# Rewriting the start of a fused retention and mixing kernel: order of the first batch's work on each engine, and idle products in TensorE's waits

## Chip, cores, metric

One core of one Trainium2 chip. The metric is the device time of one execution in microseconds (us). Executions come in states: the state "slow" is given to a run more than 1.5% above the fastest of the same kernel. For this kernel the states go with TensorE's granted clock (the share of full speed that the profile shows for it, 1 being full).

## The reference, cut to what matters

```python
# part 1: retention, B=4, H=8 heads, S=768, D=64, a state per head
state = gamma * state + k_t v_t^T ;  x_t = scale * q_t state
# part 2: x is (B, 768, 512)
theta = x @ w_theta
zr, zi = x * cos(theta), x * sin(theta)
u = x + w_tok_r @ zr + w_tok_i @ zi      # over the 768 positions
out = u + relu(u @ w_ch)
```

The kernel computes part 1 in chunks of 128 positions, 6 to a batch, 24 in all, and part 2 in tiles of 128 positions, each of which needs all six chunks of its batch.

## The kernel before: the parts in question

The first batch is special, because nothing is there yet: its six chunks are loaded and computed as three pairs (pair g = chunks 2g, 2g+1), while the weights still arrive. The helpers below say which engine does what. In the traces each of the engines that compute starts its operations in the order of these calls, even if a later one has its data: in the kernel before, pair 1's k has landed at 13.4 us, but ScalarE casts it at 17.24, after two copies that stand ahead of it.

```python
def pair_prep(g, name):     # cast / scale to bf16
    # k: ScalarE, one copy of 128x1024; q: VectorE and GpSimd, half each; v: GpSimd twice
def pair_T(g, name):        # 8 TensorE transposes into PSUM (tag "tr", 2 buffers)
    nc.vector.tensor_copy(t, ps)                     # kqT
def pair_A(g, two):         # 16 score products into at_ps (1 buffer), then
    nc.vector.tensor_mul(at, at_ps, maskp)           # masked scores
def pair_S(g, a):           # 8 products: k^T v into the state; ScalarE copies it (stbd)
def pair_I(g, a):           # 4 products: q times the state
def pair_Y(g, two):         # 16 products: scores times v
def pair_out(g, a):         # ScalarE copies yT to xT
def att_X(n):               # 4 transposes (x_sb), 4 products theta, ScalarE cos and sin
def att_Z(n):               # VectorE: z = (cos, sin) * x
def w_cast(t0): ...         # GpSimd casts two rows of w_tok (wrow, 3 buffers)
def w_tok(t0): ...          # 12 transposes, copies on VectorE (wtr) and ScalarE (wti)
def moe_M(m, lo, hi): ...   # tile m: 2 products of 128x512 for each chunk lo..hi-1
```

The schedule of the first two pairs (the third follows the same way, with the first tiles' products between):

```python
for _ in range(14):                                   # opening: TensorE kept busy
    nc.tensor.matmul(warm_ps, warm[:, 0:P], warm, start=True, stop=True)
pair_k(0); pair_q(0)                                  # pair_k = pair_prep + pair_T
pair_prep(0, "v"); pair_A(0, 0)
nc.gpsimd.tensor_copy(wth, wdma["th"])
pair_A(0, 1); pair_S(0, 0); pair_Y(0, 0); pair_S(0, 1); pair_I(0, 1); pair_Y(0, 1)
pair_out(0, 0); pair_out(0, 1)
pair_k(1); att_X(0); pair_q(1); att_X(1); att_Z(0)
pair_prep(1, "v"); pair_A(1, 0); att_Z(1); w_cast(0); pair_A(1, 1)
pair_S(1, 0); pair_Y(1, 0); pair_I(1, 0); pair_I(1, 1); pair_S(1, 1); pair_Y(1, 1)
pair_out(1, 0); pair_out(1, 1)
pair_prep(2, "k"); att_X(2); att_X(3); w_tok(0); pair_T(2, "k"); moe_M(0, 0, 2)
... (cut)
```

Of the kernel before, what the change touches and what calls it, by code (L numbers as in the profile page):

```python
# [32 lines left out]
def kernel(  # L33
# [17 lines left out]
    nc = tc.nc  # L51
    B, H, S, D = q.shape
    dm = H * D
    P = 128
# [38 lines left out]
    wdma = {}  # L93
# [90 lines left out]
    def att_prep(n):  # L184
        c = n % nT
        r3 = "p (h d) -> p h d"
        kqb = work.tile([P, 2, dm], BF, name="kqb", bufs=5)
        kb, qb = kqb[:, 0, :], kqb[:, 1, :]
        vb = work.tile([P, dm], BF, name="vb", bufs=5)
        nc.gpsimd.tensor_copy(kb.rearrange(r3, h=H), raw[n, "kf"])  # L190
        nc.gpsimd.tensor_mul(qb.rearrange(r3, h=H), raw[n, "qf"],  # L191
                             _bcast_last(qsc[:, c], D))
        nc.gpsimd.tensor_mul(vb.rearrange(r3, h=H), raw[n, "vf"],  # L193
                             _bcast_last(vsc[:, c], D))
        st[n] = dict(kqb=kqb, kb=kb, qb=qb, vb=vb)
# [20 lines left out]
    def pair_prep(g, name):  # L216
        t = work.tile([P, 2, dm], BF, name="kqb", bufs=5)
        src = raw[g, name].rearrange("p h (two d) -> p two h d", two=2)
        dst = t.rearrange("p two (h d) -> p two h d", h=H)
        if name == "k":  # L220
            nc.scalar.copy(dst, src)
        for two in range(2):
            if name == "q":
                eng = (nc.vector, nc.gpsimd)[two]
                eng.tensor_mul(dst[:, two], src[:, two],
                               _bcast_last(qscp[:, 2 * g + two], D))
            elif name == "v":
                nc.gpsimd.tensor_mul(dst[:, two], src[:, two],
                                     _bcast_last(vscp[:, 2 * g + two], D))
        st[g, name] = t  # L230

    def pair_T(g, name):
        ps = psum.tile([P, NP, 2, P], BF, name="kq_ps", tag="tr", bufs=2)
        for two in range(2):
            for j in range(NP):
                nc.tensor.transpose(ps[:, j, two, :],  # L236
                                    st[g, name][:, two, j * P:(j + 1) * P], ident)
        t = work.tile([P, NP, 2, P], BF, name="kqT", bufs=4)
        nc.vector.tensor_copy(t, ps)
        st[g, name + "T"] = t  # L240

    def pair_A(g, two):

        at_ps = psum.tile([P, 2, NP, P], FT, name="at_ps", tag="at", bufs=1)
        kT, qT = st[g, "kT"], st[g, "qT"]
        for j in range(NP):
            for a in range(2):
                half = slice(a * HP, (a + 1) * HP)
                for par in range(2):
                    rows = slice(par * D, (par + 1) * D)  # L250
                    nc.tensor.matmul(at_ps[half, par, j, :], kT[rows, j, two, half],
                                     qT[rows, j, :, half], start=(j == 0),
                                     stop=(j == NP - 1), skip_group_check=True)
        at = work.tile([P, 2, NP, P], BF, name="at", bufs=2)
        nc.vector.tensor_mul(at.rearrange("p a j t -> p (a j) t"),  # L255
                             at_ps.rearrange("p a j t -> p (a j) t"),
                             _bcast_mid(maskp[:, two].rearrange("p w i -> p (w i)"), H))
        st[g, two] = at

    def pair_Y(g, two):  # L260

        if two == 0:
            st[g, "y"] = [psum.tile([P, NP, P], FT, name="yT_ps", tag="acc", bufs=2)
                          for _ in range(2)]
        yT, at, vp = st[g, "y"], st[g, two], st[g, "v"]
        for j in range(NP):
            for a in range(2):
                half = slice(a * HP, (a + 1) * HP)
                for par in range(2):
                    h = 2 * j + par  # L270
                    nc.tensor.matmul(yT[a][par * D:(par + 1) * D, j, :],
                                     vp[half, two, h * D:(h + 1) * D],
                                     at[half, par, j, :],
                                     start=(two == 0 and j == 0),
                                     stop=(two == 1 and j == NP - 1),
                                     skip_group_check=True)

    def pair_I(g, a):

        c = 2 * g + a  # L280
        half = slice(a * HP, (a + 1) * HP)
        yT = st[g, "y"][a]
        if c > 0:
            for j in range(NP):
                nc.tensor.matmul(yT[:, j, :], stbd[c % 2][:, j, :],
                                 st[g, "qT"][:, j, :, half], start=False,
                                 stop=False, skip_group_check=True)

    def pair_out(g, a):
        c = 2 * g + a  # L290
        yT = st[g, "y"][a]
        if c == 0:
            x_tiles(0)
        xT = work.tile([P, NP, P], BF, name="xT", bufs=3)
        nc.scalar.copy(xT.rearrange("e j (i w) -> e j w i", w=2),
                       yT.rearrange("e j (w i) -> e j w i", w=2))
        st[c] = dict(xT=xT)

    def pair_S(g, a):

        c = 2 * g + a
        half = slice(a * HP, (a + 1) * HP)
        if c == 0:
            st_ps[0] = psum.tile([P, NP, P], FT, name="st_ps", tag="st", bufs=1)
        for two in range(2):
            for j in range(NP):
                nc.tensor.matmul(st_ps[0][:, j, :],  # L307
                                 st[g, "k"][half, two, j * P:(j + 1) * P],
                                 st[g, "v"][half, two, j * P:(j + 1) * P],
                                 start=(c == 0 and two == 0 and j == 0),  # L310
                                 stop=(c == nT - 2 and two == 1 and j == NP - 1),
                                 skip_group_check=True)
        state_out(0, c)
# [90 lines left out]
    def att_Z(n):  # L404
        b, c = divmod(n, nT)
        nc.vector.tensor_mul(zs[b][:, c], st[n]["cs"], _bcast_mid(xs[b][:, c, :], 2))  # L406
# [57 lines left out]
    def w_cast(t0):  # L464
        for r in range(2):
            row = work.tile([P, S], BF, name="wrow", bufs=3)
            nc.gpsimd.tensor_copy(row, wdma[r, t0])  # L467
            wrow[r, t0] = row

    def w_tok(t0):  # L470
        for r in range(2):
            w_ps = psum.tile([P, nT, P], BF, name="w_ps", tag="tr", bufs=2)
            for s0 in range(nT):
                nc.tensor.transpose(w_ps[:, s0, :],
                                    wrow[r, t0][:, s0 * P:(s0 + 1) * P], ident)
            dst = wT[r][:, :, t0 * P:(t0 + 1) * P]
            if r:
                nc.scalar.copy(dst, w_ps)  # L478
            else:
                nc.vector.tensor_copy(dst, w_ps)  # L480
# [50 lines left out]
    def pair_k(g):  # L531
        pair_prep(g, "k")
        pair_T(g, "k")

    def pair_q(g):
        pair_prep(g, "q")
        pair_T(g, "q")


    warm_ps = psum.tile([P, dm], FT, name="y_ps", tag="y", bufs=1)  # L540
    for _ in range(14):
        nc.tensor.matmul(warm_ps, warm[:, 0:P], warm, start=True, stop=True)  # L542

    pair_k(0)
    pair_q(0)
    pair_prep(0, "v")
    pair_A(0, 0)
    nc.gpsimd.tensor_copy(wth, wdma["th"])
    pair_A(0, 1)
    pair_S(0, 0)  # L550
    pair_Y(0, 0)
    pair_S(0, 1)
    pair_I(0, 1)
    pair_Y(0, 1)
    pair_out(0, 0)
    pair_out(0, 1)
    pair_k(1)
    att_X(0)
    pair_q(1)
    att_X(1)  # L560
    att_Z(0)
    pair_prep(1, "v")
    pair_A(1, 0)
    att_Z(1)
    w_cast(0)
    pair_A(1, 1)
    pair_S(1, 0)
    pair_Y(1, 0)
    pair_I(1, 0)
    pair_I(1, 1)  # L570
    pair_S(1, 1)
    pair_Y(1, 1)
    pair_out(1, 0)
    pair_out(1, 1)
    pair_prep(2, "k")
    att_X(2)
    att_X(3)
    w_tok(0)
    pair_T(2, "k")
    moe_M(0, 0, 2)  # L580
    pair_q(2)
    att_Z(2)
    pair_prep(2, "v")
    pair_A(2, 0)
    moe_M(0, 2, 3)
    att_Z(3)
    w_cast(1)
    pair_A(2, 1)
    pair_S(2, 0)
    pair_Y(2, 0)  # L590
    pair_I(2, 0)
    pair_I(2, 1)
    moe_M(0, 3, 4)
    pair_Y(2, 1)
    pair_out(2, 0)
    pair_out(2, 1)
    w_tok(1)
    att_X(4)
    w_cast(2)
    att_prep(nT)  # L600
    moe_M(1, 0, 4)
    att_X(5)
    att_Z(4)
    moe_M(0, nT - 2, nT - 1)
    moe_M(1, nT - 2, nT - 1)
    att_T(nT)
    att_Z(nT - 1)
    w_tok(2)
    moe_M(0, nT - 1, nT)
    moe_M(1, nT - 1, nT)  # L610

# [4 lines left out]
    for m in range(2, nT):  # L616
        i = 2 * (m - 2)
# [88 lines left out]
```

## Time and profile before

| | before |
|---|---|
| runs, us | 188.95, 226.11, 191.99, 189.16: median 190.57 |
| span of the profiled run (a further one, 191.03 us, fast) | 189.3 us |
| mean granted TensorE clock of it | 0.955 |
| TensorE busy, share of the span | 88% |
| first scores of the loop (chunk 6) begin | 55.96 us |
| from there to the end | 133.3 us |

Up to chunk 6's scores lies the code that the change rewrites, from there on the code is the same in both kernels. From about 70 us on TensorE is busy nearly without gaps (between 56 and 72 us it is busy for 13.7 of 16). In the first 56 us it waits, and its clock is halved for 17 us.

### The profile page before, as it was taken

To read this page: it belongs to the slowest core of one execution; us is meant where nothing else is said; L and a number is where in the kernel's file an instruction comes from. 1 tells how busy PE (TensorE), PEld (TensorE's weight loads), DVE (VectorE), ACT (ScalarE), POOL (GpSimd) and SP (SyncE) were. 2 spreads that over 40 slices of the span, in tenths; PEclk is the share of its full clock that TensorE was granted. 3 is DMA by queue.
4 is the path that set the end of the run, shared out by engine and by line. 5 is a ranking of instruction groups with operands and counts; after the bars stand their busy time and mean duration, and the time that the engine had idled before them with its cause. 6 is when DMAs were issued, how large, how long until landed. Compare 5 with 4: busy or idle time off the path is not lost.

```text
span 189.3 us, 3807 instructions
## 1 busy us (share of the span) xinstructions
PE 166.2 (88%) x1496; PEld 95.6 (51%) x1522; DVE 106.5 (56%) x150; ACT 78.9 (42%) x146; POOL 73.1 (39%) x102
## 2 busy tenths in 40 slices
PE   7645966869878969999999999999999999999991
PEld 2333544445445645565556655555555544444560
DVE  2360690482368558787875768665656544443442
ACT  6316247515414683564636453554454532200010
POOL 6375390304499879865552267205000000000000
PEclk9985596978999999999999999999999999999999
DMA  4999999299999999999989579992384334244343
GB/s 143 318 317 336 292 357 209 68 256 253 240 225 282 216 223 212 263 277 207 235 143 214 134 148 220 207 194 73 66 155 110 89 68 111 83 139 112 96 132 113
DMA packets 85907, 35.65 MB, mean 188 GB/s; under 512 B 70912, under 2 KB 80384, under 8 KB 85888
## 3 DMA queue, kind: packets, MB, share of 16 engines
q1 hardware_dynamic: 85744, 35.27, 79.8%
q8 instruction: 12, 0.20, 0.5%
q10 hardware_dynamic: 144, 0.13, 0.2%
q14 instruction: 7, 0.06, 0.1%
HBM read 25.69 MB, written 6.29 MB: 169 GB/s over the span
## 4 chain that ended last, share of the span: by engine, by line
PE 79%; DVE 8%; ACT 5%; issue 4%; DMA 2%; DVEq 0%; ACTq 0%
PE y_ps L424 29%; PE o_ps L452 10%; PE th_ps L395 10%; PE yT_ps L359 3%; PE at_ps L330 3%; PE y_ps L542 3%; PE kq_ps L202 3%; PE x_ps L392 3%; PE st_ps L367 2%; PE kq_ps L236 2%; PE st_ps L307 2%; DVE at L255 2%; PE yT_ps L348 2%; PE u_ps L435 2%; DMA uT<-u 2%
## 5 line engine op out<-in xcount | busy, mean ns | idle before, releaser
L424 PE MATMUL y_ps<-z,wti 128*128 128x512 bf16 x135 | 51.2, 379 | 1.0 <-ACT wti L478 0.2
L424 PE MATMUL y_ps<-z,wtr 128*128 128x512 bf16 x126 | 48.0, 381 | 1.4 <-DVE z L406 1.0
L400 ACT ACTIVATE cs<-th_ps,halfpi 128x512 bf16<-128x512 f32 x24 | 16.5, 687 | 38.8 <-PE th_ps L395 36.4
L406 DVE TENSOR_TENSOR z<-cs,x_sb 128x1024 bf16<-128x1024 bf16 x24 | 19.0, 793 | 15.1 <-ACT cs L401 15.1
L395 PE MATMUL th_ps<-wth,xT 128*128 128x512 bf16 x89 | 26.0, 402 | 0.7 <-issue 0.4
L334 DVE TENSOR_TENSOR at<-at_ps,mask 128x1024 bf16<-128x1024 f32 x18 | 22.0, 1221 | 6.3 <-PE at_ps L330 6.2
L452 PE MATMUL o_ps<-wch,uT 128*128 128x512 bf16 x88 | 23.1, 379 | 0.4 <-DMA uT<-u 0.2
L429 DVE TENSOR_TENSOR u<-y_ps,x_sb 128x512 bf16<-128x512 f32 x23 | 15.8, 690 | 12.0 <-PE y_ps L424 12.0
L455 DVE SCALAR_TENSOR_TENSOR ot<-o_ps,u 128x512 f32<-128x512 f32 x23 | 15.9, 692 | 10.5 <-PE o_ps L452 10.4
L193 POOL TENSOR_TENSOR vb<-vf,vsc 128x512 bf16<-128x512 f32 x18 | 19.2, 1065 | 6.3 <-PE yT_ps L359 3.6
L318 ACT CAST stbd<-st_ps 64x256 bf16<-64x256 f32 x40 | 14.6, 366 | 16.6 <-PE st_ps L307 16.1
L424 PEld LDWEIGHTS <-wti 128*128 128x128 bf16 x138 | 13.5, 98 | 15.8 <-issue 2.8
L424 PEld LDWEIGHTS <-wtr 128*128 128x128 bf16 x138 | 13.5, 98 | 13.3
L191 POOL TENSOR_TENSOR kqb<-qf,qsc 128x512 bf16<-128x512 f32 x18 | 19.6, 1086 | 1.0 <-DMA qf<-in_q_dram 1.0
L190 POOL CAST kqb<-kf 128x512 bf16<-128x512 f32 x18 | 11.4, 635 | 19.6 <-issue 10.4
L467 POOL CAST wrow<-wtok 128x768 bf16<-128x768 f32 x12 | 9.8, 824 | 19.3 <-issue 18.9
L401 ACT ACTIVATE cs<-th_ps,zerob 128x512 bf16<-128x512 f32 x24 | 16.3, 679 | 0.0
L375 ACT CAST xT<-yT_ps 128x512 bf16<-128x512 f32 x18 | 10.5, 585 | 8.7 <-PE yT_ps L359 7.4
L452 PEld LDWEIGHTS <-uT 128*128 128x128 bf16 x92 | 8.8, 98 | 10.2 <-DMA uT<-u 0.4
L395 PEld LDWEIGHTS <-xT 128*128 128x128 bf16 x96 | 9.3, 105 | 7.8 <-issue 1.8
L205 DVE COPY kqT<-kq_ps 128x1024 bf16<-128x1024 bf16 x13 | 9.0, 690 | 6.7 <-PE kq_ps L202 6.7
L398 DVE COPY x_sb<-x_ps 128x512 bf16<-128x512 bf16 x19 | 7.9, 417 | 7.2 <-PE x_ps L392 7.2
(78 smaller groups left out, 198.7 us busy)
## 6 DMA issues: line engine op xcount, KB each, us to landing
out_dram<-ot SPq DMA_DIRECT2D x23, 256.0 KB, 2.2
kf<-in_k_dram SPq DMA_DIRECT2D x18, 256.0 KB, 4.8
qf<-in_q_dram SPq DMA_DIRECT2D x18, 256.0 KB, 5.0
vf<-in_v_dram SPq DMA_DIRECT2D x18, 256.0 KB, 5.4
wtok<-in_moe_w_tok_r_dram SPq DMA_DIRECT2D x6, 384.0 KB, 5.6
wtok<-in_moe_w_tok_i_dram SPq DMA_DIRECT2D x6, 384.0 KB, 5.4
pair<-in_k_dram SPq DMA_DIRECT2D x3, 512.0 KB, 8.1
pair<-in_q_dram SPq DMA_DIRECT2D x3, 512.0 KB, 9.1
```

The costliest lines, as they stand in the source:

```text
L191: nc.gpsimd.tensor_mul(qb.rearrange(r3, h=H), raw[n, "qf"], _bcast_last(qsc[:, c], D))
L193: nc.gpsimd.tensor_mul(vb.rearrange(r3, h=H), raw[n, "vf"], _bcast_last(vsc[:, c], D))
L318: nc.scalar.copy(stbd[(c + 1) % 2][sl, :, sl], st_ps[b][sl, :, sl])
L334: nc.vector.tensor_mul(at.rearrange("p a j t -> p (a j) t"), at_ps.rearrange("p a j t -> p (a j) t"), _bcast_mid(mask, H))
L395: nc.tensor.matmul(th_ps, s["xT"][:, j, :], wth[:, j, :], start=(j == 0), stop=(j == NP - 1))
L400: nc.scalar.activation(cs[:, 0, :], th_ps, AF.Sin, bias=halfpi, scale=1.0)
L401: nc.scalar.activation(cs[:, 1, :], th_ps, AF.Sin, bias=zerob, scale=1.0)
L406: nc.vector.tensor_mul(zs[b][:, c], st[n]["cs"], _bcast_mid(xs[b][:, c, :], 2))
L424: nc.tensor.matmul(y_ps, wT[r][:, s0, t0 * P:(t0 + 1) * P], zs[b][:, s0, r, :], start=(s0 == 0 and r == 0), stop=(s0 == nT - 1 and r == 1))
L429: nc.vector.tensor_add(u, y_ps, xs[b][:, t0, :])
L452: nc.tensor.matmul(o_ps, mo[m]["uT"][:, j, :], wch[:, j, :], start=(j == 0), stop=(j == nD - 1))
L455: nc.vector.scalar_tensor_tensor(ot, o_ps, 0.0, mo[m]["u"], ALU.max, ALU.add)
```

## The change

Intent: every engine gets its instructions in the order in which their data arrive, so that none stands behind one that has to wait; and TensorE gets products of zeros, whose result nobody reads, in the waits that remain, so that the clock is not taken away.

```diff
-        nc.scalar.copy(xT..., yT...)
+        (nc.vector.tensor_copy if a else nc.scalar.copy)(xT..., yT...)
...
-    pair_k(0)
-    pair_q(0)
+    keep_busy(12)
+    pair_prep(0, "k")
+    pair_T(0, "k")
+    keep_busy(4)
+    pair_prep(0, "q")
+    pair_T(0, "q")
+    keep_busy(2)
...
-    pair_out(0, 0)
-    pair_out(0, 1)
-    pair_k(1)
-    att_X(0)
-    pair_q(1)
-    att_X(1)
-    att_Z(0)
+    pair_prep(1, "k")
+    pair_Y(0, 1)
+    pair_out(0, 0)
+    pair_out(0, 1)
+    keep_busy(1)
+    pair_T(1, "k")
+    pair_prep(1, "q")
+    att_X(0)
+    att_X(1)
+    pair_T(1, "q")
+    keep_busy(2)
     pair_prep(1, "v")
     pair_A(1, 0)
+    att_Z(0)
+    w_cast(0)
+    keep_busy(2)
+    pair_S(1, 0)
+    pair_A(1, 1)
     att_Z(1)
...
     pair_out(1, 0)
     pair_out(1, 1)
-    pair_prep(2, "k")
+    w_tok(0)
+    pair_T(2, "k")
+    pair_prep(2, "q")
     att_X(2)
     att_X(3)
-    w_tok(0)
-    pair_T(2, "k")
     moe_M(0, 0, 2)
... (pair_prep(2, "k") stands earlier, inside pair 1)
+    att_Z(3)
     w_tok(1)
...
     att_X(4)
+    att_X(5)
+    moe_M(0, 3, 4)
+    att_Z(4)
     moe_M(1, 0, 4)
+    w_tok(2)
...
     att_T(nT)
     att_Z(nT - 1)
-    w_tok(2)
```

More of the change, by code (lines that the diff above doesn't have):

```diff
@@ L294, in pair_out @@
         xT = work.tile([P, NP, P], BF, name="xT", bufs=3)
-        nc.scalar.copy(xT.rearrange("e j (i w) -> e j w i", w=2),
-                       yT.rearrange("e j (w i) -> e j w i", w=2))
+        (nc.vector.tensor_copy if a else nc.scalar.copy)(
+            xT.rearrange("e j (i w) -> e j w i", w=2),
+            yT.rearrange("e j (w i) -> e j w i", w=2))
         st[c] = dict(xT=xT)
@@ L540, with keep_busy @@
     warm_ps = psum.tile([P, dm], FT, name="y_ps", tag="y", bufs=1)
-    for _ in range(14):
-        nc.tensor.matmul(warm_ps, warm[:, 0:P], warm, start=True, stop=True)
-    pair_k(0)
-    pair_q(0)
+    def keep_busy(times):
+        for _ in range(times):
+            nc.tensor.matmul(warm_ps, warm[:, 0:P], warm, start=True, stop=True)
+    keep_busy(12)
[5 more added lines that the diff above has]
+    keep_busy(2)
     pair_prep(0, "v")
+    nc.gpsimd.tensor_copy(wth, wdma["th"])
     pair_A(0, 0)
-    nc.gpsimd.tensor_copy(wth, wdma["th"])
+    keep_busy(2)
+    pair_S(0, 0)
+    keep_busy(1)
     pair_A(0, 1)
-    pair_S(0, 0)
+    pair_S(0, 1)
     pair_Y(0, 0)
-    pair_S(0, 1)
     pair_I(0, 1)
+    keep_busy(3)
+    pair_prep(1, "k")
     pair_Y(0, 1)
@@ L556 @@
     pair_out(0, 1)
-    pair_k(1)
+    keep_busy(1)
+    pair_T(1, "k")
+    pair_prep(1, "q")
     att_X(0)
-    pair_q(1)
     att_X(1)
-    att_Z(0)
+    pair_T(1, "q")
+    keep_busy(2)
     pair_prep(1, "v")
     pair_A(1, 0)
+    att_Z(0)
+    w_cast(0)
+    keep_busy(2)
+    pair_S(1, 0)
+    pair_A(1, 1)
     att_Z(1)
-    w_cast(0)
-    pair_A(1, 1)
-    pair_S(1, 0)
     pair_Y(1, 0)
     pair_I(1, 0)
+    pair_prep(2, "k")
+    pair_S(1, 1)
     pair_I(1, 1)
-    pair_S(1, 1)
+    keep_busy(1)
     pair_Y(1, 1)
@@ L574 @@
     pair_out(1, 1)
-    pair_prep(2, "k")
+    w_tok(0)
+    pair_T(2, "k")
+    pair_prep(2, "q")
     att_X(2)
     att_X(3)
-    w_tok(0)
-    pair_T(2, "k")
     moe_M(0, 0, 2)
-    pair_q(2)
+    pair_T(2, "q")
+    pair_prep(2, "v")
     att_Z(2)
-    pair_prep(2, "v")
     pair_A(2, 0)
     moe_M(0, 2, 3)
-    att_Z(3)
     w_cast(1)
@@ L592 @@
     pair_I(2, 1)
-    moe_M(0, 3, 4)
     pair_Y(2, 1)
@@ L596 @@
     pair_out(2, 1)
+    att_Z(3)
     w_tok(1)
-    att_X(4)
     w_cast(2)
     att_prep(nT)
+    att_X(4)
+    att_X(5)
+    moe_M(0, 3, 4)
+    att_Z(4)
     moe_M(1, 0, 4)
-    att_X(5)
-    att_Z(4)
+    w_tok(2)
     moe_M(0, nT - 2, nT - 1)
```

## The prediction

> **What bounds the kernel now.** I read the page first: the busy shares, the 40 slices and the chain of work that ended last.
>
> ```profile
> span 189.3 us, 3807 instructions
> ...
> PE   7645966869878969999999999999999999999991
> ...
> PEclk9985596978999999999999999999999999999999
> ...
> PE 79%; DVE 8%; ACT 5%; issue 4%; DMA 2%; DVEq 0%; ACTq 0%
> ```
>
> Each digit is a slice of 4.7 us. From about slice 15 (70 us) TensorE is at 9 to the end: the chain there is TensorE's own work, and the change touches none of it. The first 56 us are different: TensorE is at 4 to 9, and its clock is not always granted in full. Only there can this change win, and what it wins is the shift of the moment when the steady part begins. I take as that moment the end of the first six products of tile 2 (the first tile of the loop), 55.9 us in the timeline.
>
> Second, the busy time in stretches of 3.41 us (the granted clock changes at these borders, read from the trace: 6.20, 13.02, 23.26, 30.09, 33.50, 40.33, 43.74 us). Columns: stretch, length, busy us with counts of PE, PEld, DVE, ACT, POOL, clock, DMA share, GB/s.
>
> ```profile
> 9.61:13.02 3.41, 1.33 (x44) 0.98 (x43) 2.23 (x3) 0.00 (x0) 2.72 (x3) 1.00 1.15 323
> 13.02:16.43 3.41, 2.75 (x45) 1.97 (x44) 0.85 (x1) 1.82 (x5) 1.57 (x2) 0.50 1.20 299
> ...
> 30.09:33.50 3.41, 2.96 (x13) 1.72 (x15) 0.83 (x2) 2.50 (x5) 0.00 (x0) 0.50 0.80 190
> 33.50:36.91 3.41, 2.86 (x27) 1.60 (x25) 1.66 (x4) 2.38 (x4) 1.60 (x2) 1.00 0.11 15
> ...
> 40.33:43.74 3.41, 3.41 (x49) 2.49 (x49) 1.76 (x2) 0.73 (x2) 0.00 (x0) 0.50 1.10 288
> ```
>
> TensorE runs at half clock in 13.02-23.26, 30.09-33.50 and 40.33-43.74, 17.1 us in all. Also, DMA stands nearly idle (15 GB/s) in 33.50-36.91.
>
> Third, TensorE's waits up to 72 us: few large ones, all on the other engines' small steps.
>
> ```profile
> PE at_ps L251 <- DVE at L255: 3.5, 3, 1.4
> PE kq_ps L236 <- ACT kqb L221: 2.3, 1, 2.3
> PE kq_ps L236 <- DVE kqb L225: 1.8, 2, 1.6
> PE at_ps L251 <- DVE kqT L239: 1.6, 2, 0.8
> ```
>
> Fourth, the timeline, for arrivals: what the data would allow against when the kernel uses it.
>
> ```profile
> 15.29 1.04 POOL L225 TENSOR_TENSOR kqb<-pair,qscp 128x512 bf16<-128x512 f32 x1 [1.74 <-DMA pair<-in_q_dram]
> ...
> 17.24 1.05 ACT L221 CAST kqb<-pair 128x1024 bf16<-128x1024 f32 x1
> 18.35 1.03 PE L236 MATMUL kq_ps<-ident,kqb 128*128 128x128 bf16 x8 [2.31 <-ACT kqb L221]
> ...
> 25.71 1.45 DVE L406 TENSOR_TENSOR z<-cs,x_sb 128x1024 bf16<-128x1024 bf16 x1
> ...
> 38.45 0.68 DVE L406 TENSOR_TENSOR z<-cs,x_sb 128x1024 bf16<-128x1024 bf16 x1
> ```
>
> Pair 1's k was issued at 5.23 us and took 8.2 us to land (13.4), yet ScalarE casts it at 17.24, behind both xT copies. Pair 2's q half on GpSimd starts at 23.89, and its v follows, done at 28.06, yet its transposed q is made only at 37.18. So the data are there up to nine microseconds before their use: this phase is bound by order, not by arrival.
>
> **What the Trainium skill says.** (1) "TensorE: Matmul & The Clock Gate", Part 1 (the HAM clock gate): half clock by default, full clock after about one busy window of 3.4 us, lost again after idle. The trace agrees: grants last multiples of 3.41 us, the opening products come every 0.43 us and then every 0.21 us. It does not tell how full a window must be: 13.02-16.43 is 2.75 us busy and stays at half, 30.09-33.50 is 2.96 us busy and is followed by full. (2) Same page, Part 1, the engine queue depths: ScalarE and VectorE are strict FIFO. Hence a cast behind two copies waits for them, as at 17.24. (3) "SBUF - State Buffer", "Who interferes with whom": a VectorE instruction with two SBUF inputs contends with GpSimd's reads. The trace agrees: z is 1.45 us beside GpSimd's v (25.57) and 0.68 us at 38.45 with GpSimd idle.
>
> **The change part by part.**
>
> *Idle products.* 14 become 12 at the start, and 18 go into waits: 4, 2, 2, 1, 3, 1, 2, 2, 1. At full clock 18 x 0.213 = 3.8 us (at half clock 7.7). In the list below almost all fall into waits. What they can save: half of the TensorE work on the chain that ran at half clock. From the chain in order of time: 2.2 us (13.92-16.09), 4.3 us (18.35-24.2, its part at half clock), 3.2 us (30.32-33.5), 3.1 us (40.33-43.74): 12.8 us, half is 6.4 us at most, and less, since a faster TensorE soon waits for VectorE.
>
> *Order.* Walked by hand with durations from the rows: transposes of 8 0.45 us, score or Y group 0.34, S 0.45, theta of 4 0.86; k cast 1.04, xT 0.66-0.73, stbd pair 0.76, cs pair 1.27; kqT 0.69 (next one 0.6 later), q half 0.87-1.34, at 1.22, z 0.68 or 1.2 beside GpSimd.
> - Pair 0: q transposed 8.72 (was 8.89), scores 10.12, S ahead of the second scores at 11.0 because v is done at 10.96, last Y 14.05-14.4 at full clock (was 15.40-16.04). Gain 1.6 us.
> - Pair 1: k cast at 13.75-14.8, between stbd and xT; transposed at 14.85 (was 18.35). The second xT is on VectorE beside the first on ScalarE, which saves about 0.65 us in each pair. q is multiplied at 16.05, after its arrival at 15.2; both X follow, q transposed at 17.7 (was 21.75), v done 19.2 by its arrival, S at 19.75 (was 26.20), last Y at about 23.6 (was 28.59). Gain 5 us.
> - Pair 2: k lands at about 22, q at 23.9. wtok tile 0 transposed at 23.6-24.3 (was 34.04). q transposed at 28.5 (was 37.18), scores at 29.8 (was 38.58): gain 8.7 us. xT done at 35.1 (was 45.8): gain 10.7, of which the clock gives some 1.5.
> - Tail: here the new order costs. VectorE does z of chunk 3 (35.15-36.3) before it empties the first w_ps (36.9), and the next transposes need that PSUM buffer: TensorE waits some 2 us near 35-37. It then does X(4), X(5), the rest of tiles 0 and 1, and waits again for z of chunk 5 behind kqT (to 45.1), then for u of tile 0. Tile 2's six products end at 47.75. Gain 55.9 - 47.75 = 8.1 us if the clock stays full.
>
> Off that sum: low activity in 33.5-36.9 (about 1.4 us of work in 3.4) may cost one window at half clock during X(4) and X(5), some 1.5 us; and jitter and extra issue steps that a hand list leaves out, some 0.3 us. That leaves about 6.4 us. Starting TensorE's clock two products earlier gives 0.2 us and is in the list.
>
> *Steady part.* It must keep up with a start 6 to 8 us earlier. GpSimd's copies of wtok 1 no longer wait for TensorE until 34.66, so w3's load is issued at about 29-30 instead of 35.52 and the DMA hole closes, some 4 to 5 us of transfer. Chunk 7's k and q are ready 1.7 us before their transposes, 8's 3.5 us, 9's 3.7 us, and from chunk 10 on over 9 us (timeline, GpSimd's end against the transposes at 56.29, 60.68, 64.96, 73.29). With transfers 4 to 5 us earlier and TensorE 6 to 8 us earlier, 8 and 9 still just fit.
>
> Sum: 191.0 (the profiled execution's own time) - 6.4 = 184.6; the fastest of the three runs before, 188.95, gives 182.6. I say **184.0 us**.
>
> **Rivals.**
> - *The idle products stand in the way.* They are in program order, so one placed before a group whose input is ready delays it, and at half clock each costs 0.43 us. For it: if the clock is lost once (the windows run free, so a start at another phase can lose it), 18 of them cost up to 7.7 us, a good part on the chain. Against it: they sit mostly where the trace before shows 0.8 to 1.5 us of waiting. It would leave a gain of 2 to 4 us: 187 to 189.
> - *The bound passes to transfers and GpSimd.* For it: DMA is near full from 36 to 95 us and GpSimd 100% busy in 55-65. Then the early gain is given back around chunks 8 to 10, down to what the closed DMA hole gives, 4 to 5 us: 186 to 187. Against it: GpSimd's idle time after 45 us is mostly TensorE-paced (8.75 us before 45.02), and this moves along.
> - *The clock stays full and everything fits:* all 8 us or a little more, 181 to 183.
> - *Only order matters,* the clock is as bad as before: about 4 us, 187.
>
> **Range and chances.** The main path and the third rival span 181-185, the other three 186-189; I give the former two thirds. Executions of the same kernel differ by 1.5% before (188.95 and 191.99, with 226.11 as an outlier), probably from the clock's phase. Range 180.5 to 188.0. Faster by over 2% needs more than 3.8 us: 0.84; within 2%: 0.13; slower: 0.03.
>
> **What would show it.** Right: full clock in nearly all windows from 7 to 34 us, pair 1's k cast near 14 us, pair 2's q transposed near 28.5 us, no DMA hole near 33 us, tile 2's six products ending near 48 us, and the rest as long as before (133 us). Wrong: half clock in two or more windows before 35 us with idle products on the chain; TensorE waiting for DMA or GpSimd at the transposes of chunks 7 to 9; a wait of much more than 2 us at the transposes of chunk 4.

## The result

| | before | changed |
|---|---|---|
| runs, us | 188.95, 226.11, 191.99, 189.16 | 181.78, 183.34, 181.50, 181.83 |
| median | 190.57 | 181.81 |
| span of the profiled run, its clock | 189.3, 0.955 | 180.0, 0.994 |
| chunk 6's scores begin | 55.96 | 46.90 |
| from there to the end | 133.3 | 133.1 |

The ratio is 0.9633, with a 95% interval of 0.9541 to 0.9725. It is the mean time of one kernel's fast runs over that of the other's of the same rounds, so it is not quite the ratio of the medians quoted here (which is 0.954: of the four runs before only 188.95 and 189.16 are fast, 191.99 is slow, and 226.11 is an outlier whose cause is not known). The change is faster. By fast runs it gains 189.06 - 182.11 = 6.9 us. Between the two profiled runs it is more, since that of the kernel before is one of its longer fast ones (191.03 us, clock 0.955, where runs of 188.5 to 189.5 us have 0.958 to 0.960).

The last two rows say where the time came from: of the 9.3 us between the two spans, 55.96 - 46.90 = 9.1 us lie before chunk 6's scores. From there on the two take equally long.

The page of the changed kernel, the lines that answer to those of before:

```profile
span 180.0 us, 3837 instructions
...
PE   7889886796989699999999999999999999999990
...
PEclk9999999999999999999999999999999999999997
...
PE 82%; DVE 6%; ACT 5%; issue 3%; DVEq 0%; ACTq 0%
```

The clock row has no dip until the last slice. In stretches of 3.41 us (this run's clock windows have a border at 7.20, that of the kernel before at 6.20, though the first product begins at 1.26 and 1.25: the grid does not follow the start of the kernel; columns: length, busy us and counts of PE, PEld, DVE, ACT, POOL, clock, DMA share, GB/s):

```profile
10.61:14.03 3.42, 3.09 (x60) 2.16 (x58) 2.45 (x2) 1.47 (x5) 2.15 (x2) 1.00 1.20 298
...
27.68:31.09 3.41, 2.04 (x31) 1.27 (x28) 2.06 (x3) 1.37 (x3) 2.51 (x4) 1.00 1.11 216
31.09:34.50 3.41, 2.64 (x67) 1.80 (x66) 2.00 (x2) 0.73 (x2) 0.00 (x0) 1.00 1.03 284
34.50:37.92 3.42, 2.48 (x29) 1.76 (x27) 2.87 (x5) 1.97 (x3) 2.82 (x4) 1.00 1.28 245
```

Transfers run at 245 GB/s where the kernel before had its hole of 15 GB/s. TensorE's waits up to 72 us (total, times, longest):

```profile
PE y_ps L425 <- DVE z L407: 2.1, 2, 1.5
...
PE at_ps L251 <- DVE kqT L239: 1.5, 3, 0.8
...
PE at_ps L251 <- DVE at L255: 0.8, 2, 0.5
...
PE kq_ps L236 <- DVE kqb L225: 0.5, 1, 0.5
```

The wait for the k cast (2.3 us before) is gone, the one for q fell from 1.8 to 0.5 us. A part of that is only renamed: a wait that holds idle products no longer shows as idle. New is a long one for z, 1.47 us until 44.13 us (before, the longest for z was 0.6). The timeline shows the moves, first ScalarE, then TensorE:

```profile
14.02 1.04 ACT L221 CAST kqb<-pair 128x1024 bf16<-128x1024 f32 x1
15.09 0.73 ACT L295 CAST xT<-yT_ps 128x512 bf16<-128x512 f32 x1
```

```profile
15.12 0.62 PE L236 MATMUL kq_ps<-ident,kqb 128*128 128x128 bf16 x8
...
18.06 0.61 PE L236 MATMUL kq_ps<-ident,kqb 128*128 128x128 bf16 x8
...
23.54 0.84 PE L475 MATMUL w_ps<-ident,wrow 128*128 128x128 bf16 x12
24.90 0.61 PE L236 MATMUL kq_ps<-ident,kqb 128*128 128x128 bf16 x8 [0.52 <-DVE wtr L481]
...
28.38 0.61 PE L236 MATMUL kq_ps<-ident,kqb 128*128 128x128 bf16 x8
```

The k cast of pair 1 stands at 14.02 (was 17.24), ahead of the copy of xT; its transposes at 15.12 (was 18.35). The last line is pair 2's q, 28.38 (was 37.18): the 9 us are gained by then.

### The profile page after: what moved, and what is told of

The parts are those of the page before. It is cut to its first block, busy times and chain, and to the rows that moved or that the text cites. A ratio compares the mean times of both kernels' runs of the same rounds, so it can differ in the third digit from the quotient of the medians.

```text
span 180.0 us, 3837 instructions
## 1 busy us (share of the span) xinstructions
PE 163.8 (91%) x1511; PEld 93.6 (52%) x1538; DVE 107.8 (60%) x153; ACT 77.3 (43%) x143; POOL 74.6 (41%) x102
## 4 chain that ended last, share of the span: by engine, by line
PE 82%; DVE 6%; ACT 5%; issue 3%; DVEq 0%; ACTq 0%
PE y_ps L425 31%; PE o_ps L453 11%; PE th_ps L396 11%; PE yT_ps L360 3%; PE at_ps L331 3%; PE y_ps L545 3%; PE kq_ps L202 3%; PE st_ps L368 3%; PE x_ps L393 2%; PE yT_ps L349 2%; PE kq_ps L236 2%; PE u_ps L436 2%; PE y_ps L495 1%; ACT stbd L319 1%; DVE at L255 1%
## 5 line engine op out<-in xcount | busy, mean ns | idle before, releaser
L401 ACT ACTIVATE cs<-th_ps,halfpi 128x512 bf16<-128x512 f32 x24 | 16.5, 687 | 35.1 <-PE th_ps L396 32.8
L396 PE MATMUL th_ps<-wth,xT 128*128 128x512 bf16 x90 | 24.0, 379 | 0.3
L396 PEld LDWEIGHTS <-xT 128*128 128x128 bf16 x96 | 8.6, 98 | 6.8
L545 PE MATMUL y_ps<-warm 128*128 128x512 bf16 x26 | 9.7, 497 | 1.5 <-DVE warm L124 1.3
```

Of the source, the lines that this page charges most:

```text
L396: nc.tensor.matmul(th_ps, s["xT"][:, j, :], wth[:, j, :], start=(j == 0), stop=(j == NP - 1))
L401: nc.scalar.activation(cs[:, 0, :], th_ps, AF.Sin, bias=halfpi, scale=1.0)
```

## The experiments

Twelve kernels ran on three chips, all correct, each beside new runs of the kernel before. The fast runs of before averaged 189.2, 189.8 and 189.4 us, and 189.1 with the changed kernel, so times are compared to about 0.5 us. Only the change itself and e12 have the verdict "faster"; the other experiments, each with three or four fast runs, have "unclear", and what follows rests on their medians, clocks and markers. "Marker" is the start of chunk 6's scores in the profiled run, "rest" the span minus it, "clock" the mean clock of the profiled run. The profiled run of e1 is slow, that of e4 its longest; medians take in the slow runs (one each in e1, e3, e6 and e7).

| kernel | median us (range) | ratio to before | clock | marker | rest |
|---|---|---|---|---|---|
| before | 190.57 (188.95-226.11) | 1 | 0.955 | 55.96 | 133.3 |
| changed | 181.81 (181.50-183.34) | 0.963 | 0.994 | 46.90 | 133.1 |
| e1 order only | 183.39 (182.71-185.51) | 0.967 | 0.963 | 50.16 | 133.6 |
| e2 idle products only | 186.89 (186.32-187.40) | 0.987 | 0.988 | 52.21 | 132.9 |
| e3 xT on ScalarE | 181.19 (181.16-183.93) | 0.957 | 0.998 | 46.46 | 132.9 |
| e4 two swaps in the tail | 180.52 (180.25-182.43) | 0.955 | 0.976 | 46.96 | 133.7 |
| e5 k behind xT | 183.55 (182.92-184.01) | 0.967 | 1.000 | 48.20 | 133.6 |
| e6 q behind x | 182.98 (181.62-187.25) | 0.960 | 0.985 | 48.10 | 133.5 |
| e7 transfer hole closed in before | 193.30 (191.07-194.38) | 1.014 | 0.935 | 58.62 | 133.5 |
| e8 swaps and zero products | 180.04 (179.50-180.75) | 0.949 | 0.995 | 44.63 | 133.2 |
| e9 wtok behind X | 182.84 (182.68-183.10) | 0.965 | 1.000 | 47.78 | 133.4 |
| e10 pair 1's middle | 183.82 (182.56-185.13) | 0.970 | 0.991 | 48.51 | 133.6 |
| e11 idle products doubled | 182.86 (182.55-183.87) | 0.966 | 0.999 | 47.70 | 133.4 |
| e12 e8 with xT on ScalarE | 179.94 (179.64-180.47) | 0.950 | 1.000 | 45.45 | 133.0 |

The rest is between 132.9 and 133.7 us in all fourteen profiles, while the marker goes from 44.6 to 58.6: whatever is won or lost before chunk 6 goes to the end undiminished.

### e1 and e2: order alone, idle products alone

e1 is the changed kernel with all `keep_busy` lines removed but the opening 12. e2 is the kernel before with `keep_busy` in its own waits:

```diff
-    pair_k(0)
-    pair_q(0)
+    pair_k(0)
+    keep_busy(4)
+    pair_q(0)
+    keep_busy(2)
     pair_prep(0, "v")
     pair_A(0, 0)
+    keep_busy(4)
...  (1 after pair_Y(0, 0), 8 before pair_k(1), 4 after pair_A(1, 0), 4 before pair_prep(2, "k"))
```

> The changed kernel with its 18 idle products taken out (the 12 at the start stay); order as changed. Theory (order gives most, the clock about a fifth to a third): the clock is lost in some windows again, granted mean about 0.96, time 183.5 to 185.5, that is 5 to 7 us below the kernel before. Rival A (the idle products give most): 186 us or more. Rival B (the clock gives nothing, the new order alone keeps it full or it does not matter): 181 to 182.5 and clock above 0.985.

> The kernel before, in its old order, with 27 idle products in its waits of the first 30 us (none once tile 0 holds their PSUM buffer). Theory: the window 13.02-23.26 becomes full clock and the time falls by 1 to 3 us, to 187 to 188.5. Rival A (the idle products give most of the 8.8 us): 184 us or less. Rival B (they only stand in the way): 190 us or more.

e1: three fast runs of 182.71 to 183.61 us at clocks of 0.966 to 0.981, and the slow one that was profiled, 185.51 at 0.963. The fast runs of the kernel before had 0.951 to 0.960, so with the new order the clock is lost in some windows, but in fewer. e2: 186.32 to 187.40, a little faster than expected. By fast runs e1 is 3.3% (6.3 us) below the kernel before, e2 1.35% (2.6 us), the whole change 3.7% (6.9 us). Rival A falls in both: neither part alone gives it all. The two may overlap, 6.3 + 2.6 being more than 6.9 (a better order leaves fewer waits in which the clock can be lost), but each figure has about 1.5 us of noise either way, so that is not shown. On top of the new order the idle products are worth about 1 us by fast runs (183.16 - 182.11; 1.6 by medians). The times of the two kernels overlap, their clocks do not: 0.981 at most in e1, 0.986 at least in the changed kernel. In the old order the idle products, 27 there and in longer waits, are worth 2.6 us. That both kernels are at nearly full clock makes e2 against the changed kernel the fairest view of order: marker 52.21 against 46.90, 5.3 us, of which e2's one window at half clock is a part.

That window shows how the clock is lost (stretches of 3.41 us of e2):

```profile
30.64:34.05 3.41, 2.74 (x29) 1.58 (x27) 1.85 (x3) 1.93 (x4) 1.60 (x2) 1.00 0.95 221
34.05:37.46 3.41, 1.68 (x42) 1.28 (x42) 3.37 (x5) 0.00 (x0) 0.00 (x0) 1.00 0.95 223
37.46:40.88 3.42, 3.06 (x48) 2.17 (x48) 0.81 (x1) 1.07 (x3) 0.00 (x0) 0.50 0.91 241
```

One window with TensorE busy for 1.68 of 3.41 us, just where e2 has no idle products any more, and the next runs at half clock.

### e5, e6, e9, e10, e3: the order, one piece at a time

Each takes one piece of the new order back and keeps the rest.

e5: the k casts of pairs 1 and 2 behind the xT copies.

```diff
-    pair_prep(1, "k")
     pair_Y(0, 1)
     pair_out(0, 0)
     pair_out(0, 1)
+    pair_prep(1, "k")
...  (the same for pair 2)
```

> The changed kernel with the k casts of pairs 1 and 2 put behind the xT copies of the pair before, as they were in the old order. Theory (the order of ScalarE was the largest single piece in pair 1): pair 1's k is transposed about 1 us later, pair 2's about 1 us, the steady part starts 1 to 2 us later: 182.5 to 184. Rival (k is not on the path any more since the q half ends last): 181.2 to 182.

Measured 183.55, 1.7 us over the changed kernel, as expected. The wait that the change had removed is back in TensorE's list:

```profile
PE kq_ps L236 <- ACT kqb L221: 3.3, 3, 1.4
```

e6: q multiplied where the old order had it.

```diff
     pair_T(1, "k")
-    pair_prep(1, "q")
     att_X(0)
+    pair_prep(1, "q")
+    pair_T(1, "q")
     att_X(1)
-    pair_T(1, "q")
...  (pair 2: pair_prep(2, "q") behind moe_M(0, 0, 2))
```

> The changed kernel with the q multiplications of pairs 1 and 2 put back behind the x_sb copies and the products as in the old order. Theory (VectorE strictly in order: q then waits for xT, the transposes and x_sb): q's transposes of pair 1 1 to 1.5 us later and of pair 2 1.5 to 2 us later, partly on the same path: 183.5 to 185.5. Rival (only the idle products and k's place count): 181.2 to 182.5.

The run with full clock takes 181.62 us, the same as the changed kernel; the others (clocks 0.985, 0.985, 0.963) take 182.7 to 187.3, the last being slow. The expectation fails. Pair 1's q is transposed at 17.26 in it, earlier than the 18.06 of the changed kernel, and pair 2's at 28.28 against 28.38: TensorE is busy with X groups and products until then, so a later q is hidden. Its profiled run lost the clock only from 32.8 to 36.2 us, after a low window; whether this order loses it more often, four runs do not settle.

```profile
29.40:32.80 3.40, 1.73 (x41) 1.18 (x41) 2.88 (x4) 0.00 (x0) 0.95 (x2) 1.00 0.96 218
32.80:36.20 3.40, 3.40 (x55) 2.61 (x53) 1.82 (x3) 1.46 (x3) 0.05 (x1) 0.50 1.19 296
36.20:39.60 3.40, 2.51 (x22) 1.45 (x20) 1.75 (x4) 1.72 (x3) 3.40 (x4) 1.00 1.11 291
```

e9: w_tok(0) and pair 2's k transposes behind the X groups.

```diff
-    w_tok(0)
-    pair_T(2, "k")
     pair_prep(2, "q")
     att_X(2)
     att_X(3)
+    w_tok(0)
+    pair_T(2, "k")
```

> The changed kernel with wtok tile 0's transposes (and the transposes of pair 2's k behind them) put back behind the two X groups of pair 1, where the old order had them; q of pair 2 is multiplied where it was. Theory (they fill TensorE's wait for the xT copies; in the old order with idle products that stretch, last Y of pair 1 to pair 2's q transposes, took 6.7 us against 4.8): the steady part starts 1.3 to 2 us later: 183.0 to 183.8. Rival (the place of k's cast is the whole order gain): 181.3 to 182.

182.84, 1.0 us more at full clock: a real piece, smaller than expected. TensorE then waits for xT with nothing to do, as its timeline shows:

```profile
23.15 0.42 PE L271 MATMUL yT_ps<-at,kqb 64*64 64x128 bf16 x16
24.55 0.40 PE L393 MATMUL x_ps<-ident,xT 128*128 128x128 bf16 x4 [0.98 <-ACT xT L295]
```

e10: z ahead of the masked scores, second scores ahead of S in pair 1.

```diff
+    att_Z(0)
     pair_A(1, 0)
-    att_Z(0)
+    att_Z(1)
     w_cast(0)
     keep_busy(2)
-    pair_S(1, 0)
     pair_A(1, 1)
-    att_Z(1)
+    pair_S(1, 0)
     pair_Y(1, 0)
...  (and pair_I(1, 1) ahead of pair_S(1, 1))
```

> The changed kernel with the middle of pair 1 in the old order on VectorE and TensorE: z of chunks 0 and 1 ahead of the masked score copies, the second scores ahead of S, S of the second half behind the state product. Theory (z ahead of at delays the one score buffer by up to 0.6 us twice; the old order took 4.9 us from the first scores to the last Y against 4.1): 0.5 to 1.2 us more, 182.2 to 183. Rival: the same as the changed kernel, 181.3 to 182.

183.82, more than expected. By its profiled run 0.9 us of that is the order: pair 2's q is transposed at 29.30 against 28.38, at full clock in both. The rest is a window at half clock, 46.23 to 49.64, right at the start of the chunk loop; the window ahead of it has TensorE busy for only 1.59 us (the waits for z and, behind it, for u, which lie in two windows in the changed kernel, fall into one here). Where the waits fall in the grid differs from run to run, and its runs spread from 182.6 to 185.1.

e3: both xT copies on ScalarE.

```diff
-        (nc.vector.tensor_copy if a else nc.scalar.copy)(
+        nc.scalar.copy(
```

> The changed kernel with both xT copies of a pair on ScalarE again. Theory: each pair's second xT is done 0.6 to 0.7 us later on the path, in two or three pairs: 182.8 to 184. Rival (VectorE has no room, the split is only moved work): 181.3 to 182.3, the same as the changed kernel.

Three runs of 181.16 to 181.23 and a slow one of 183.93 (clock 0.981): no slower. The split is worth nothing. In e3 ScalarE's two copies of pair 0 run from 14.82 to 16.15, and TensorE takes the second only at 16.70, after the first X group, which lasts about 1.1 us:

```profile
14.82 1.33 ACT L295 CAST xT<-yT_ps 128x512 bf16<-128x512 f32 x2
```

```profile
15.61 0.40 PE L393 MATMUL x_ps<-ident,xT 128*128 128x128 bf16 x4
15.84 1.03 PE L396 MATMUL th_ps<-wth,xT 128*128 128x512 bf16 x4
16.70 0.39 PE L393 MATMUL x_ps<-ident,xT 128*128 128x128 bf16 x4
```

So the order's gain has at least three sources, k's cast (1.3 to 1.7 us), the middle of pair 1 (0.9) and wtok in the wait for xT (0.9 to 1.0); q's place and the split give none. The sum, 3 to 3.6 us, is short of the 5.3 between e2 and the changed kernel, and the half-clock window of e2 accounts for some of what is missing; the remainder is not divided further. The new order inside pair 0 and that of the stretch after pair 2 were not taken back alone.

### e11: do idle products stand in the way?

Every `keep_busy(n)` after the opening becomes `keep_busy(2 * n)`.

> The changed kernel with each of its nine groups of idle products doubled (36 for 18). Theory (the counts are cut to the waits; what is above stands in the way, 0.213 us each at full clock): 1 to 3 us more, 182.8 to 184.8, and the clock full in every run. Rival (waits have room, TensorE is nowhere near the bound in this phase): 181.3 to 182.

182.86, 1.0 us more, with the clock full or nearly so in all runs (0.985 to 0.999). 18 more products are 18 x 0.213 = 3.8 us of TensorE time; about a quarter comes through to the end. The chosen counts fit the waits; products too many cost less than their own time, and e1 shows that none at all cost about as much (1.0 us by fast runs, 1.6 by medians).

### e7: is it the transfers?

```diff
-            row = work.tile([P, S], BF, name="wrow", bufs=3)
+            row = work.tile([P, S], BF, name="wrow", bufs=4)
```

in the kernel before.

> The kernel before with one more wrow buffer (4 for 3), nothing else: GpSimd can copy wtok 1 at about 29 us and the loads behind it are issued some 5 us earlier, so the hole in the transfers at 33 to 36 us closes. Theory (transfers are not the bound in this phase): same time as before within 0.5 us, 188.5 to 192 by state. Rival (the closed hole is where the gain comes from): 3 us or more below before.

The stretch 33 to 36 us, in the kernel before and then in e7:

```profile
33.00:36.00 3.00, 2.69 (x26) 1.54 (x24) 1.15 (x3) 2.69 (x5) 1.34 (x2) 0.92 0.01 2
```

```profile
33.00:36.00 3.00, 2.69 (x23) 1.65 (x22) 0.98 (x2) 2.27 (x4) 0.58 (x1) 0.81 1.05 278
```

The hole is closed, 278 GB/s for 2, and no time is won: 191.1 to 194.4 us, above the range expected. By medians it is even slower than the kernel before, with lower clocks (0.927 to 0.954); that is not clear of noise (interval 0.999 to 1.029), and why it would lose more windows stays open. The closed hole is not where the gain comes from. Whether the changed kernel could have done without it was not tried.

### e4, e8, e12: the waits that the change left

e4 is the changed kernel with two swaps.

```diff
-    att_Z(3)
     w_tok(1)
+    att_Z(3)
...
-    att_T(nT)
     att_Z(nT - 1)
+    att_T(nT)
```

> The changed kernel with two swaps: wtok tile 1's transposes and copies ahead of z of chunk 3, and z of chunk 5 ahead of the transposes of chunk 6, so that the wait of 1.47 us for z at 44.1 us should go. Theory (TensorE's start of the steady part sets the end): 1 to 1.6 us less, 180.2 to 180.8. Rival (GpSimd or transfers bound the steady part by now, and the gain comes back as a wait at chunks 7 to 9): 181.5 to 182.

Three runs at 180.25 to 180.58, 1.2 us less, and a fourth, the profiled one, at 182.43 with a clock of 0.976. The wait for z fell from 2.1 to 0.3 us:

```profile
PE y_ps L425 <- DVE z L407: 0.3, 1, 0.3
```

That one lost the clock from 32.15 to 38.98:

```profile
28.74:32.15 3.41, 1.76 (x42) 1.14 (x40) 2.56 (x3) 0.38 (x1) 2.16 (x3) 1.00 0.76 156
32.15:35.57 3.42, 3.42 (x53) 2.63 (x53) 1.57 (x2) 1.12 (x3) 0.00 (x0) 0.50 1.04 280
35.57:38.98 3.41, 3.18 (x21) 2.14 (x20) 2.16 (x4) 1.24 (x3) 2.95 (x4) 0.50 0.97 201
```

e8 therefore adds 8 idle products to e4 after 29 us. Tile 0 holds their PSUM bank by then, so they are added to its sum, with weights of zero:

```diff
+    def add_zero(times):
+        for _ in range(times):
+            nc.tensor.matmul(mo[0]["y"], warm[:, 0:P], warm, start=False, stop=False)
...
     pair_T(2, "q")
+    add_zero(2)
...  (1 after pair_A(2, 0), 2 after moe_M(0, 2, 3), 3 after w_tok(1))
```

> The two swaps of e4_tail, and 8 more idle products in the waits between 29 and 36 us. Their PSUM bank is held by tile 0 by then, so they add zero to tile 0's sum (weights zero, no start, no stop). Theory (the runs of 182 to 183 us lose the clock in one or two windows after 32 us): every run keeps full clock, 180.0 to 180.6, none above 181. Rival (the lost window does not come from low activity there): one run in four at 182 or more still, or the products delay the path and all are 0.5 us slower.

179.50 to 180.75, every clock at 0.994 or more, where e4's had gone down to 0.976 and the changed kernel's to 0.986. By median it gains 0.5 us on e4, which alone would be within noise. In its profile the matching windows are fuller and stay at full clock:

```profile
29.20:32.61 3.41, 2.94 (x62) 1.79 (x61) 2.89 (x4) 0.07 (x1) 1.77 (x2) 1.00 0.92 189
32.61:36.03 3.42, 3.19 (x61) 2.12 (x50) 2.42 (x5) 2.19 (x4) 1.37 (x2) 1.00 1.03 303
```

e12 is e8 with both xT copies on ScalarE (the line of e3).

> e8_tail_zero with both xT copies on ScalarE again. In e3_xT_scalar that was 181.2 against 181.5 to 181.8 with the split, so the split is worth nothing or less there; theory: the same here, 179.3 to 180.2. Rival (in the tail VectorE is freed less than ScalarE is loaded): 180.3 to 181.

Six runs, 179.64 to 180.47: the same as e8, within what four and six runs can tell; here too every clock is at 0.998 or more. Both are some 5% below the kernel before and 1% below the changed kernel.

## Why the prediction was right

- **Where time can be won.** The prediction held that only the stretch before the loop counts, and that its end moves the end of the kernel one for one. Right: the rest stayed within 132.9 to 133.7 us over fourteen profiles.
- **The walk by hand.** Right to within a microsecond, mostly to less than 0.4: pair 1's k transposed 14.85 predicted, 15.12 measured; its q 17.7 and 18.06; pair 2's q 28.5 and 28.38; its scores 29.8 and 29.77; tile 2's six products ending 47.75 and 46.97. The tail was taken 0.8 us too long: X(4) does not wait for VectorE's wtr copy (36.9) but for ScalarE's wti, done earlier, and starts at 36.20, after a wait of 0.89 us where about 2 had been forecast.
- **The deductions.** 1.5 us for a half-clock window near 37 us was one too many for most runs: three of the four have a clock of 0.994 or more, and only the run of 183.34 us (0.986) is longer by that much. Between the profiled executions, which the walk compares, 191.0 - 181.8 = 9.2 us were gained where 6.4 had been forecast; the 0.8, the 1.5 and the 0.3 taken off for jitter are most of the difference. That 6.4 lies so near the 6.9 of the fast runs is in part luck, since what was taken off did not come and the profiled run of before was one of the longer ones. The risk was real, but lay earlier: TensorE is busy for 2.48 us of 34.50-37.92, not 1.4 of 3.4, since it waits for less; where the clock was lost, in e4's run of 182.43 us and e6's profiled one, it followed a low window at 28.74-32.15 and at 29.40-32.80. None of the ten runs of e8 and e12 shows such a loss.
- **Attribution.** Only in part right. The k cast is the largest piece that was found (e5). The split of the xT copies was put down as saving about 0.65 us in each pair; e3 shows nothing saved, since the second copy is hidden behind the first X group. The walk also counted on q being multiplied at its arrival; e6 shows that it could be later.
- **Rivals.** Idle products in the way: no, taking them out costs 1.0 to 1.6 us, doubling them 0.9 to 1.0. Only order, with the clock as bad as before, 187: e1 shows 183.2 (fast runs), and its clock is better than before too. The bound passing to transfers and GpSimd: GpSimd does wait for transfers now, 2.3 us in sum between 30 and 60 us, but TensorE between 44 and 75 us waits for neither, as predicted from the slack of chunks 7 to 9; w3's loads are issued at 29.27 and 30.31, where 29 to 30 was predicted. The hole in the transfers, on which this rival put 4 to 5 us, is worth nothing alone (e7). The rival that came true is the third, full clock and everything fits, 181 to 183: the prediction had it, but left its own number above it. None of the signs of being wrong that it named was seen.

## What to carry to other kernels

When the steady part of a kernel is bound by one engine without gaps, look for the moment at which it begins, and walk the stretch ahead of it by hand with the trace's durations: the earliest time that data allow against the time of use, engine by engine. Put a copy that unlocks the next chain ahead of copies that only finish the last one, and independent transposes into the wait between them. Fill what waits remain on TensorE with products of zeros, counted to the wait; where no free PSUM bank is left, adding zero to an open sum does it too.

## What the Trainium skill lacked or had wrong

- "TensorE: Matmul & The Clock Gate", Part 1 (the HAM clock gate), gives idle gaps of about 3.4 us as what loses the clock. Here no gap was that long (the longest wait in the kernel before is 2.3 us): half of one 3.41 us window was enough. Windows busy for 1.58 us (before, 36.91-40.33), 1.59 us (e10), 1.68 us (e2), 1.73 us (e6, 29.40-32.80) and 1.76 us (e4) were followed by half clock; windows of 1.95 us (changed, 41.33-44.75) and 2.04 us (changed, 27.68-31.09) were not. There is no sharp border in busy time: 2.11 us (before, 26.67-30.09) was followed by half clock, and 1.74 us (before, 6.20-9.61) was not. The same Part tells of a kernel that lost the clock through many short idle times ("A second HAM failure mode: psum-queue depth-cycling"), as here; how full a window has to be, it does not say.
- The same Part has the full clock back after about one busy window. Here that did not always hold: e4's window 32.15-35.57 is busy for 3.42 us and is followed by half clock, while e2's 37.46-40.88 with 3.06 us was followed by full clock. The kind of product does not explain it: e6's window 32.80-36.20, busy for 3.40 us with the same groups of products as e4's (those of pair 2's S, Y and I, and w_tok's transposes), was followed by full clock. So the busy time that the profile models does not settle when the clock comes back, and what does stays open.
- No page speaks of products of zeros to keep the clock, or of putting them into the bank of an open accumulation: 8 of them with zero weights, without start and stop, left the result correct and cost nothing that shows (e8).
- "VectorE: DVE Perf Modes" sets ScalarE closer to PSUM in its specifications. For the copy of 128x512 f32 from PSUM to bf16 it made no difference here: 0.73 us on ScalarE, 0.73 us on VectorE.
